# Two attention blocks on one core: operands turned and K rows spread by DMAs instead of by engines

## The chip, the cores and the metric

The kernel runs on one core of a Trainium2 chip. The metric is the device time of one execution in microseconds; the figure given is the median of three runs. A profile is one further execution, recorded by the hardware profiler. Engines are called PE (TensorE), ACT (ScalarE), DVE (VectorE), POOL (GpSimd) and SP (SyncE, which here only issues DMAs).

## The reference

Two independent blocks work on inputs of 2048 rows by 512 columns, with 32 heads of 16 columns each, everything in bfloat16. Their results stand side by side in one output of 2048 by 1024.

```python
# both: qkv = x @ wqkv, split into q, k, v of 32 heads x 16 columns
# A: linear attention
phi = lambda t: where(t > 0, t + 1, exp(t)) + 1e-6
kv  = einsum("bhsd,bhse->bhde", phi(k), v);  z = einsum("bhsd->bhd", phi(k))
o   = (phi(q) @ kv) / (phi(q) @ z + 1e-6)
a   = o @ wo
# B: softmax attention over all 2048 keys
p   = softmax(q @ k.T * 0.25);  o = p @ v
b   = o @ wo
out = concatenate([a, b], axis=-1)
```

B needs 32 heads x 2048 x 2048 exponentials. In tiles of 128 keys by 512 queries these are 2048 blocks. A is much smaller and is fitted in beside B.

## The kernel before

The program is laid out by a planner that runs when the kernel is built: it keeps a clock for each engine with a booked duration for every operation, and picks what can start first. What comes out is a fixed instruction sequence for each engine with semaphore waits. Constants such as `TEND` (the length the planner spreads its side jobs over), `ALAG` (how far A's jobs may lag before DVE gets no more exponential blocks) and `DBL` (how much work may wait for DVE) steer it.

B's scores are made with four heads at once, each in a quarter of the PE's rows. K is kept twice, once with the rows of the even heads and once with those of the odd heads, the other rows zero. A block's exponential is either computed by ACT from the scores in PSUM (three or two blocks in one instruction), or by DVE in four steps on the bits of a 16-bit number, after which PV takes two matmuls instead of one:

```python
# L670: scores of one block; KM is the masked K: [row, group % 2, even/odd, key]
return e.matmul(dst, lhsT=KM[32*g:32*g+32, Gp % 2, e_, j*128:(j+1)*128],
                rhs=QT[32*g:32*g+32, Gp % 2, c*512:(c+1)*512], ...)
# L816: ACT's way, w = 1536 or 1024
e.activation(PT[:, row, c0:c0+w], SCR[sl][:, 0:w], ACTF.Exp, scale=SC)
# L756, L872, L873, L874: DVE's way; DI for each block, the rest for three blocks at once
e.tensor_scalar(DI..., DB..., ESC, EB, op0=ALU.mult, op1=ALU.add)
e.tensor_scalar(Q, I, 0x3FF, 0x3800, op0=ALU.bitwise_and, op1=ALU.bitwise_or)
e.tensor_tensor(Qh, Ih, Qh, op=ALU.mult)
e.tensor_scalar(I, I, 0xFC00, 8, op0=ALU.bitwise_and, op1=ALU.bitwise_or)
```

The parts that the change touches, in the version before. x of both blocks comes in with rows on partitions and is turned by PE against an identity, then copied out of PSUM. A's x is turned in two halves inside the room of KNa (`XSA`), the second half loaded when the first is done:

```python
def xT_stages(src, keys_, dst, dname, t0, n=2, lane="dve"):
    def tr(e, bk):
        for i in range(n):
            for cc in range(4):
                ins = e.transpose(bfv(bk)[:, ...], src(t0+i)[:, cc*128:(cc+1)*128], identb[:])
        return ins
    return [("pe", 4*n*TRB, f_pe(tr, ...)),
            (lane, 0.36*n, f_ev(lane, copy_to(lane, ..., ...), [], [...]))]     # L419, xTb or xTa
```

The first projections (K, then Q of group 0) read the turned x of the first four row tiles; K of group 0 is masked by DVE straight from PSUM (L466). For the later groups DVE copies the projection to KR and POOL multiplies it by the two masks:

```python
st.append(("dve", 0.7, ... e.tensor_copy(KR[:, kr, :], f32v(bk)) ...))                 # L474
for e_ in range(2):
    st.append(("pool", 0.7, ... e.tensor_scalar(KM[:, r, e_, cs], KR[:, kr, :],
                                                PAR[:, e_:e_+1], None, op0=ALU.mult) ...))  # L476
st.append(("dve", 0.62, ... e.tensor_reduce(KMX[:, i:i+1], KR[:, kr, :], ...) ...))     # L478
```

A's output of a row tile is divided into OA, turned by PE, copied to ONT, and multiplied by WO; B's output tiles use the same last step without a turn:

```python
# anum_job, L593: OA[:, o2] = numerator * RD            (DVE)
# otr_job:  PE turns OA into PSUM; L419: ONT = copy       (PE, DVE)
# omm_job, L619: four matmuls with WOa or WOb; L419: copy to OB (A) or spare rows of KNa (B);
#           L623: store
early += [xjob(4), xjob(6), proj_job(0, 1, 1, fast=True), xjob(8), ...]   # the start, shortened
```

At the start PE runs matmuls on the identity to warm up (`warm`, 28 of them, L985). DVE also adds up two bounds from which a flag decides whether a slower general path follows; with these inputs it doesn't run.

Of the kernel before, what the change touches and what calls it, by code (L numbers as in the profile page):

```python
# [219 lines left out]
def bass_concat_heads__linear_attn_block__softmax_full_mha__prompt_kernel(nc, A_x, A_wqkv, A_wo, B_x, B_wqkv, B_wo, out):  # L220
# [17 lines left out]
    TEND = 780.0  # L238
    ALAG = 20.0
    DLEAD = 0.5  # L240
    DBL = 6.0
# [8 lines left out]
    with es:  # L250
# [30 lines left out]
        ONT = sb("ONT", [128, 1, 512], BF)  # L281
        OB = sb("OB", [128, 1, 512], BF)
        OA = sb("OA", [128, 2, 512], BF)
# [37 lines left out]
        xbn = B_x[0].rearrange("(t p) c -> p t c", p=128)  # L321
        xan = A_x[0].rearrange("(t p) c -> p t c", p=128)
        on_keys = lambda t: [("ON", t, g) for g in range(8)]
        load(ON[:, 0:2, :], xbn[:, 0:2, :], on_keys(0) + on_keys(1))
        load(ON[:, 2:4, :], xbn[:, 2:4, :], on_keys(2) + on_keys(3), queue="act")
        load(Wb[:, :, 0:128], wbv[:, :, 0:128], [("Wb", 0, 0)])
        load(Wb[:, :, 512:640], wbv[:, :, 512:640], [("Wb", 1, 0)], queue="act")
        for t0 in range(4, NT, 4):
            load(ON[:, t0:t0 + 4, :], xbn[:, t0:t0 + 4, :], sum([on_keys(t) for t in range(t0, t0 + 4)], []))
            if t0 == 4:  # L330
                load(Wb[:, :, 1024:1536], wbv[:, :, 1024:1536], [("Wb", 2)])
        load(Wb[:, :, 128:512], wbv[:, :, 128:512], [("Wb", 0, g) for g in range(1, NGP)])
        load(Wb[:, :, 640:1024], wbv[:, :, 640:1024], [("Wb", 1, g) for g in range(1, NGP)])
        XSA = KNa[:, :, :].rearrange("p (a b) n -> p a (b n)", b=2)
        kst = lambda i: [("KNa", 2 * i), ("KNa", 2 * i + 1)]
        for t0 in range(0, 8, 4):
            load(XSA[:, t0:t0 + 4, :], xan[:, t0:t0 + 4, :], sum([kst(i) for i in range(t0, t0 + 4)], []))
# [4 lines left out]

        def mk_ident(t, key):
            sch.add("pool", lambda e: e.memset(t[:], 0.0), writes=[key])
            sch.add("pool", lambda e: e.affine_select(out=t[:], in_=t[:], compare_op=ALU.not_equal, fill=1.0,
                                                      base=0, pattern=[[-1, 128]], channel_multiplier=1),
                    reads=[key], writes=[key])
# [3 lines left out]
        sch.add("dve", lambda e: e.memset(PVb[:], 0.0), writes=[("PV", g) for g in range(4)])  # L351
        def band(t, n, rep, key):
# [8 lines left out]
        for e_ in range(2):  # L361
            sch.add("dve", lambda e, e_=e_: e.tensor_reduce(PAR[:, e_:e_ + 1], ZMk[:].rearrange("p (a e) -> p e a", e=2)[:, e_, :],
                                                           axis=AX.X, op=ALU.max),
                    reads=["ZMk"], writes=[("PAR", e_)])
        for Gp_ in range(NGP):
# [50 lines left out]
        MM, TRB, TRF = 0.26, 0.085, 0.29  # L416
# [4 lines left out]

        def xT_stages(src, keys_, dst, dname, t0, n=2, lane="dve"):
            def tr(e, bk):
                for i in range(n):
                    for cc in range(4):
                        ins = e.transpose(bfv(bk)[:, (i * 4 + cc) * 128:(i * 4 + cc + 1) * 128],
                                          src(t0 + i)[:, cc * 128:(cc + 1) * 128], identb[:])
                return ins
            return [("pe", 4 * n * TRB, f_pe(tr, keys_ + ["identb"])),
                    (lane, 0.36 * n, f_ev(lane, copy_to(  # L430
                        lane, lambda: dst[:, :, t0 * 128:(t0 + n) * 128].rearrange("p c (i n) -> p i c n", n=128),
                        lambda bk: bfv(bk)[:, 0:n * 512].rearrange("p (i c n) -> p i c n", c=4, n=128)),
                        [], [(dname, t) for t in range(t0, t0 + n)]))]
# [14 lines left out]
        def proj_job(Gp, sc, kind, fast=False, **kw):  # L448
# [15 lines left out]
            if fast:  # L464
                for e_ in range(2):
                    st.append(("dve", 0.75, f_ev("dve", lambda e, bk, e_=e_: e.tensor_scalar(KM[:, r, e_, cs], f32v(bk), PAR[:, e_:e_ + 1], None, op0=ALU.mult),  # L466
                                                 [("PAR", e_)], [("KM", r, e_, sc)])))
                st.append(("dve", 1.2, f_op("dve", lambda e: e.tensor_reduce(KMX[:, i:i + 1], KM[:, r, :, cs], axis=AX.XY, op=ALU.max,
                                                                            apply_absolute_value=True),
                                            [("KM", r, e_, sc) for e_ in range(2)], [("KMX", i)])))  # L470
# [4 lines left out]
            for e_ in range(2):  # L475
                st.append(("pool", 0.7, f_op("pool", lambda e, e_=e_: e.tensor_scalar(KM[:, r, e_, cs], KR[:, kr, :], PAR[:, e_:e_ + 1], None, op0=ALU.mult),  # L476
                                             [("PAR", e_), ("KR", kr)], [("KM", r, e_, sc)])))
            st.append(("dve", 0.62, f_op("dve", lambda e: e.tensor_reduce(KMX[:, i:i + 1], KR[:, kr, :], axis=AX.X, op=ALU.max,  # L478
                                                                         apply_absolute_value=True), [("KR", kr)], [("KMX", i)])))
            return Job(st, needs, [(3, ("K", Gp, 0, sc)), (4, ("K", Gp, 1, sc)), (5, ("KMX", i))], rel=2, **kw)  # L480
# [59 lines left out]
        def akv_job(t, hp, **kw):  # L540
# [8 lines left out]
            return Job(st, [("xTa", t)] + ([("akv", hp - 1, bl) for bl in range(2)] if hp else [("xTa", t_) for t_ in range(NT)]),  # L549
# [34 lines left out]
        def anum_job(sc, tl, **kw):  # L584
            pq = sc % 2
            o2 = tl % 2
            def f(e, bk):
                for bq in range(4):
# [6 lines left out]
                            RD[:, pq, tl * 32:tl * 32 + 32].unsqueeze(2).broadcast_to([128, 32, 16]), op=ALU.mult), [("RD", pq)], [("OA", o2)]))],  # L595
                       [("aden", sc)] + ([("atr", sc, tl - 2)] if tl >= 2 else ([("atr", sc - 1, tl + 2)] if sc else [])),
                       [(0, ("anum", sc, tl)), (1, ("oa", sc, tl))], **kw)


        out_lanes = [sch.new_dma_lane() for _ in range(5)]  # L600
        stores = []
        KNf = KNa[:, :, :].rearrange("p (s b) n -> p s (b n)", b=2)
        obf = lambda o2: OB[:, 0, :] if o2 == 0 else KNf[:, o2 - 1, :]
        obk = lambda o2: [("OB", 0)] if o2 == 0 else kst(o2 - 1)

        def otr_job(src, keys, needs, gives, **kw):
            def tr(e, bk):
                for hb in range(4):
                    ins = e.transpose(bfv(bk)[:, hb * 128:(hb + 1) * 128], src[:, hb * 128:(hb + 1) * 128], identb[:])
                return ins  # L610
            return Job([("pe", 4 * TRB, f_pe(tr, list(keys) + ["identb"])),
                        ("dve", 0.43, f_ev("dve", copy_to("dve", lambda: ONT[:, 0, :], lambda bk: bfv(bk, 512)), [], [("ONT", 0)]))],
                       needs, gives, **kw)

        def omm_job(ab, t, o2, needs, gives, lane="dve", **kw):
            WO, wkey, col0 = (WOa, "WOa", 0) if ab == "a" else (WOb, "WOb", 512)
            def mm(e, bk, hb):
                src = ONT[:, 0, hb * 128:(hb + 1) * 128] if ab == "a" else ON[:, 4 * hb + t // 4, (t % 4) * 128:(t % 4 + 1) * 128]
                return e.matmul(f32v(bk), lhsT=src, rhs=WO[:, hb, :], start=(hb == 0), stop=(hb == 3))  # L619
            ins_ = [("ONT", 0)] if ab == "a" else sum([on_keys(4 * hb + t // 4) for hb in range(4)], [])  # L620
            def fin(bk):
                sch.add(lane, lambda e: copy_to(lane, lambda: obf(o2), lambda bk: f32v(bk))(e, bk), reads=[bk[3]], writes=obk(o2))
                stores.append(sch.add(out_lanes[o2], lambda e: e.dma_start(out[0][t * 128:(t + 1) * 128, col0:col0 + 512], obf(o2)),  # L623
                                      reads=obk(o2), queue="sp", force_signal=True))
            return Job(halves(mm, ins_ + [wkey]) + [(lane, 0.7 if lane == "dve" else 0.6, fin)],
                       needs + ([("akv", 1, bl) for bl in range(2)] if o2 else []), gives, **kw)
# [46 lines left out]
        def qk_reads(bl):  # L673
            res = []
            for u, j, g in bl:
                Gp, c, e_ = unit(u)
                res += [("QT", Gp % 2, c), ("KM", Gp % 2, e_, j // 4)]
# [26 lines left out]

        def d_pick(at, used):
# [3 lines left out]
            if bi is None or u is None or dfree[bi] > at or d_backlog(at) > DBL or (ajobs and at > ajobs[0].ready + ALAG):  # L709
# [248 lines left out]
        def unit_done(u, t_):  # L958
# [17 lines left out]
            if Gp == NGP - 1 and e_ == 1:  # L976
                fin = u == NU - 1
                for tl in range(4):
                    ln = ("dve", "act")[tl % 2] if fin else "dve"
                    urgent2.append(omm_job("b", 4 * c + tl, 1 + tl, [("on", Gp, c)], [(1, ("st", c, tl))], lane=ln))  # L980


        def warm(e):
            for i_ in range(28):
# [3 lines left out]
        xsrc = lambda t: ON[:, t, :]  # L988

# [5 lines left out]
        for t in range(4):  # L995
            now(Job(xT_stages(xsrc, on_keys(t), xTb, "xTb", t, 1, ("dve", "act")[t % 2]), gives=[(1, ("xTb", t))]), SBANKS[t], 7.0)
# [4 lines left out]
        now(jk, SBANKS[4], 10.5)  # L1001
        now(jq, DBANK[0], 11.0)
        for k_ in T:
            T[k_] = 10.3
        T["act"] = 11.2
        afree[:] = [10.0, 10.0]
        dfree[:] = [11.2, 9.0]
# [4 lines left out]
        def xjob(t):  # L1012
            return Job(xT_stages(xsrc, on_keys(t) + on_keys(t + 1), xTb, "xTb", t), gives=[(1, ("xTb", t)), (1, ("xTb", t + 1))])
        early += [xjob(4), xjob(6), proj_job(0, 1, 1, fast=True), xjob(8), xjob(10), v4_job(0, 0), proj_job(0, 2, 1, fast=True), xjob(12), xjob(14),
                  v4_job(1, 0), proj_job(0, 3, 1, fast=True), v4_job(2, 0), v4_job(3, 0)]
# [15 lines left out]
        for h2 in range(2):  # L1031
            for i in range(0, 8, 2):
                t = 8 * h2 + i
                st = xT_stages(lambda tt, h2=h2: XSA[:, tt - 8 * h2, :], kst(i) + kst(i + 1), xTa, "xTa", t)
                if h2 == 0 and i == 6:
                    fn0 = st[0][2]
                    def f2(bk, fn0=fn0):
                        fn0(bk)
                        for t0 in range(0, 8, 4):
                            load(XSA[:, t0:t0 + 4, :], xan[:, 8 + t0:12 + t0, :], sum([kst(i_) for i_ in range(t0, t0 + 4)], []))  # L1040
                    st[0] = (st[0][0], st[0][1], f2)
                ajobs.append(Job(st, [("xTa", 7)] if h2 else [], [(1, ("xTa", t)), (1, ("xTa", t + 1))]))
# [173 lines left out]
```

## Time and profile before

| what | value |
|---|---|
| median of three runs | 792.77 us (792.19 to 793.15) |
| span of the profiled execution | 791.8 us |
| first exponential on ACT starts | 9.83 us |
| last exponential on ACT ends | 778.51 us |
| POOL's mask products (L476) | 24, mean 1725 ns |
| DMA traffic | 13.51 MB, 302 GB/s in the first fortieth of the span, 17 GB/s over all |
| A's stores | 16, from 361 to 711 us |

A line of groups reads: line, engine, operation, what is written and read, shapes, count, then the total busy time and the mean of one in ns, then the idle time of the engine before them and who ended it. A line of waits reads: who waited for whom, total us, times, longest. The chain that ended last is followed backwards from the last instruction to whatever released each step; its shares say where the time that counts was spent. An engine that is busy most of the span matters only where the chain runs through it.

### The profile page before, as it was taken

The numbers are of one execution on the slowest core, as the hardware profiler recorded it, in microseconds if no ns is written. First come the engines' busy times: TensorE is split into PE (matmuls) and PEld (weight loads), VectorE is DVE, ScalarE is ACT, GpSimd is POOL, SyncE is SP. The second block draws the span as 40 slices with busy tenths as digits, with TensorE's granted clock in tenths as the row PEclk, the third lists the DMA queues.
The fourth block names the chain that finished last, engine by engine and source line by source line (L and its number), as shares of the span: only waits on it lengthen the run. The fifth ranks groups of instructions, "written<-read, shape, count | busy, mean of one in ns | idle before, by whom it ended". The sixth has DMA issues, their size and how long they took to land.

```text
span 791.8 us, 13394 instructions
## 1 busy us (share of the span) xinstructions
PE 674.2 (85%) x5585; PEld 209.6 (26%) x5634; DVE 723.3 (91%) x1264; ACT 760.0 (96%) x706; POOL 45.9 (6%) x43
## 2 busy tenths in 40 slices
PE   7889999898988888988888788988877888888875
PEld 4322333333322322222222222222222222222211
DVE  6999999989999999999999989999999997989992
ACT  6899999999999999999999999999999999999993
POOL 2000011300000001310000001121000000000000
PEclk9999999999999999999998999999999899999997
DMA  9201100000000000000000000000000000010000
GB/s 302 71 1 28 27 1 1 1 2 2 1 1 1 1 2 1 2 1 14 7 8 1 1 8 15 7 1 2 13 7 8 1 14 21 14 34 1 22 7 31
DMA packets 13139, 13.51 MB, mean 17 GB/s; under 512 B 1808, under 2 KB 12560, under 8 KB 13072
## 3 DMA queue, kind: packets, MB, share of 16 engines
q1 hardware_dynamic: 12272, 12.19, 4.8%
q8 instruction: 46, 0.75, 0.4%
q10 hardware_dynamic: 800, 0.39, 0.2%
q14 instruction: 21, 0.17, 0.1%
HBM read 8.39 MB, written 4.19 MB: 16 GB/s over the span
## 4 chain that ended last, share of the span: by engine, by line
ACT 72%; DVE 15%; PE 12%; issue 1%; POOL 0%; ACTq 0%; POOLq 0%
ACT PT L816 70%; PE pPV L935 5%; DVE DI L756 4%; PE pS L670 4%; DVE DQ L873 2%; DVE DQ L872 1%; ACT EA L534 1%; DVE DI L874 1%; PE pD L619 1%; PE pD L450 1%; DVE QMX L461 1%; DVE KMX L478 0%; DVE PQT L537 0%; DVE OT L962 0%; DVE KR L474 0%
## 5 line engine op out<-in xcount | busy, mean ns | idle before, releaser
L816 ACT ACTIVATE PT<-pS 128x1536 f16<-128x1536 f32 (+1 forms) x651 | 750.9, 1380 | 13.6 <-PE pS L670 6.5
L670 PE MATMUL pS<-QT,KM 32*128 32x512 bf16 x1628 | 256.2, 391 | 83.9 <-ACT PT L816 79.4
L756 DVE TENSOR_SCALAR DI<-pD 128x512 int16<-128x512 f32 x414 | 281.0, 689 | 29.3 <-PE pD L670 25.5
L935 PE MATMUL pPV<-PT,VV 128*17 128x512 f16 x1628 | 225.6, 390 | 1.4 <-ACT PT L816 1.0
L670 PE MATMUL pD<-QT,KM 32*128 32x512 bf16 x420 | 154.3, 392 | 2.2 <-DVE DI L756 1.1
L670 PEld LDWEIGHTS pS<-QT,KM 32*128 32x128 bf16 x1628 | 61.9, 91 | 329.1 <-ACT PT L816 299.4
L873 DVE TENSOR_TENSOR DQ<-DI,DQ 128x1536 f16<-128x1536 f16 x140 | 134.0, 957 | 2.3
L935 PE MATMUL pPV<-DQ,VV 128*17 128x512 f16 x420 | 117.0, 390 | 1.3 <-DVE OT L962 1.3
L935 PE MATMUL pPV<-DI,VV 128*17 128x512 f16 x420 | 116.2, 387 | 0.0
L872 DVE TENSOR_SCALAR DQ<-DI 128x1536 int16<-128x1536 int16 x140 | 78.4, 560 | 1.6
L874 DVE TENSOR_SCALAR DI<-DI 128x1536 int16<-128x1536 int16 x140 | 77.8, 556 | 2.0 <-DVE DQ L873 0.8
L476 POOL TENSOR_SCALAR KM<-KR,PAR 128x512 bf16<-128x512 bf16 x24 | 41.1, 1725 | 489.4 <-DVE KR L474 489.4
L935 PEld LDWEIGHTS pPV<-PT,VV 128*17 128x17 bf16 x1628 | 46.2, 88 | 85.0 <-issue 70.2
L670 PEld LDWEIGHTS pD<-QT,KM 32*128 32x128 bf16 x420 | 36.2, 91 | 14.9 <-DVE DI L756 7.0
L543 PE MATMUL pD<-Wa,xTa 128*128 128x256 bf16 x256 | 38.1, 277 | 2.1 <-DVE DI L756 1.8
L450 PE MATMUL pD<-xTb,Wb 128*128 128x512 bf16 x103 | 31.5, 390 | 6.0 <-issue 2.0
L935 PEld LDWEIGHTS pPV<-DI,VV 128*17 128x17 bf16 x420 | 30.4, 92 | 21.2 <-issue 2.0
L935 PEld LDWEIGHTS pPV<-DQ,VV 128*17 128x17 bf16 x420 | 25.9, 89 | 26.1 <-issue 16.3
L534 ACT ACTIVATE EA<-pD 128x256 bf16<-128x256 f32 (+1 forms) x48 | 29.9, 622 | 0.0
L962 DVE STREAM_TRANSPOSE OT<-pPV 128x512 f32<-128x512 f32 x32 | 22.7, 709 | 7.1 <-PE pPV L935 6.9
L543 PEld LDWEIGHTS pD<-Wa,xTa 128*128 128x128 bf16 x256 | 20.6, 98 | 18.6 <-DVE DI L756 7.2
L619 PE MATMUL pD<-WOb,ON 128*128 128x512 bf16 x57 | 18.7, 440 | 5.4 <-DVE ON L973 3.7
(86 smaller groups left out, 349.1 us busy)
## 6 DMA issues: line engine op xcount, KB each, us to landing
KNa<-in_A_x_dram SPq DMA_DIRECT2D x4, 512.0 KB, 6.7
out_dram<-OB SPq DMA_DIRECT2D x16, 128.0 KB, 1.7
out_dram<-KNa SPq DMA_DIRECT2D x16, 128.0 KB, 1.7
ON<-in_B_x_dram SPq DMA_DIRECT2D x3, 512.0 KB, 7.7
Wa<-in_A_wqkv_dram SPq DMA_DIRECT2D x1, 1536.0 KB, 12.2
Wb<-in_B_wqkv_dram SPq DMA_DIRECT2D x2, 384.0 KB, 8.5
Wb<-in_B_wqkv_dram SPq DMA_DIRECT2D x1, 512.0 KB, 6.8
WOb<-in_B_wo_dram SPq DMA_DIRECT2D x1, 512.0 KB, 12.2
```

Of the source, the lines that this page charges most:

```text
L450: return e.matmul(f32v(bk), lhsT=Wb[:, cc, kind * 512 + Gp * 128:kind * 512 + Gp * 128 + 128], rhs=xTb[:, cc, sc * 512:(sc + 1) * 512], st ...
L476: st.append(("pool", 0.7, f_op("pool", lambda e, e_=e_: e.tensor_scalar(KM[:, r, e_, cs], KR[:, kr, :], PAR[:, e_:e_ + 1], None, op0=ALU.m ...
L534: ("act", 0.1 + n * 0.00085, f_ev("act", lambda e, bk: e.activation(EA[:, q, 0:n], f32v(bk)[:, c0:c0 + n], ACTF.Exp), [], [("EA", q)])),
L543: return e.matmul(f32v(bk)[:, 256 * k_:256 * k_ + 256], lhsT=xTa[:, cc, t * 128:(t + 1) * 128], rhs=Wa[:, cc, 512 + 512 * k_ + 256 * hp:51 ...
L619: return e.matmul(f32v(bk), lhsT=src, rhs=WO[:, hb, :], start=(hb == 0), stop=(hb == 3))
L670: return e.matmul(dst, lhsT=KM[32 * g:32 * g + 32, Gp % 2, e_, j * 128:(j + 1) * 128], rhs=QT[32 * g:32 * g + 32, Gp % 2, c * 512:(c + 1) ...
L756: sch.add("dve", lambda e: e.tensor_scalar(DI[:, buf, i * 512:(i + n) * 512], DB[:, bi * 512:(bi + n) * 512], ESC, EB, op0=ALU.mult, op1=A ...
L816: sch.add("act", lambda e: e.activation(PT[:, row, c0:c0 + w], SCR[sl][:, 0:w], ACTF.Exp, scale=SC), reads=skeys(sl), writes=[("PT", row, ...
L872: (0.07 + w * 0.00027, lambda e: e.tensor_scalar(Q, I, 0x3FF, 0x3800, op0=ALU.bitwise_and, op1=ALU.bitwise_or), ik, qk_),
L873: (0.07 + w * 0.00053, lambda e: e.tensor_tensor(Qh, Ih, Qh, op=ALU.mult), ik + qk_, qk_),
L874: (0.07 + w * 0.00027, lambda e: e.tensor_scalar(I, I, 0xFC00, 8, op0=ALU.bitwise_and, op1=ALU.bitwise_or), ik, ik)]
L935: sch.add("pe", lambda e, g=g, j=j, h=h, P=P, first=first, last_=last_: e.matmul(PVb[32 * g:32 * g + 17, 0:512], lhsT=VV[:, j, vcol(h):vco ...
```

## The change

x of both blocks no longer passes through PE and PSUM: transposing DMAs write it turned from HBM to SBUF, 512 rows at a time. This takes away the transposes, their copies on DVE and ACT, and the jobs that held PSUM banks for them. A's attention output is turned by a transposing DMA from SBUF to SBUF. The masked K of the later groups is filled by DMAs that copy only the 16 rows each head needs, eight for a projection, into a KM whose other rows are zeroed once at the start by POOL. ONT, OB and OA lose their own memory: they lie in KNa and VNa, which are free when A's sums are done. The planner's constants follow.

```diff
-    TEND = 780.0
-    ALAG = 20.0
+    TEND = 765.0
+    ALAG = 30.0
-    DBL = 6.0
+    DBL = 5.0
...
-        ONT = sb("ONT", [128, 1, 512], BF)
-        OB = sb("OB", [128, 1, 512], BF)
-        OA = sb("OA", [128, 2, 512], BF)
...
+        def load_t(dst, dname, x, t0, n):
+            lane = sch.new_dma_lane()
+            sch.add(lane, lambda e: e.dma_start_transpose(dst[:, :, t0 * 128:(t0 + n) * 128], x[0][t0 * 128:(t0 + n) * 128, :]),
+                    writes=[(dname, t) for t in range(t0, t0 + n)], queue="sp")
         load(Wb[:, :, 512:640], wbv[:, :, 512:640], [("Wb", 1, 0)], queue="act")
+        load(Wb[:, :, 0:128], wbv[:, :, 0:128], [("Wb", 0, 0)], queue="act")
+        load_t(xTb, "xTb", B_x, 0, 4)
+        load_t(xTb, "xTb", B_x, 4, 4)
+        load(Wb[:, :, 1024:1536], wbv[:, :, 1024:1536], [("Wb", 2)])
+        load_t(xTb, "xTb", B_x, 8, 4)
+        load_t(xTb, "xTb", B_x, 12, 4)
...
+        for t0 in range(0, NT, 4):
+            load_t(xTa, "xTa", A_x, t0, 4)
...
+        for r_, e_, sc_ in zeros:
+            sch.add("pool", lambda e, r_=r_, e_=e_, sc_=sc_: e.memset(KM[:, r_, e_, sc_ * 512:(sc_ + 1) * 512], 0.0), ...)
...
-            for e_ in range(2):
-                st.append(("pool", 0.7, f_op("pool", lambda e, e_=e_: e.tensor_scalar(KM[:, r, e_, cs], KR[:, kr, :], PAR[:, e_:e_ + 1], None, op0=ALU.mult),
+            def spread(bk):
+                for e_ in range(2):
+                    for g in range(4):
+                        rows = slice(32 * g + 16 * e_, 32 * g + 16 * e_ + 16)
+                        sch.add(km_lanes[4 * e_ + g], lambda e, rows=rows, e_=e_: e.dma_start(KM[rows, r, e_, cs], KR[rows, kr, :]),
+                                reads=[("KR", kr)], writes=[("KM", r, e_, sc, g)], queue="sp")
+            st.append(("pool", 5.0, spread))
...
+        def ont_load(o2):
+            sch.add(ont_lane, lambda e: e.dma_start_transpose(ONT[:, o2, :].rearrange("p (c n) -> p c n", n=128), OA[:, o2, :]),
+                    reads=oak(o2), writes=kst(6 + o2), queue="sp")
...
         def warm(e):
-            for i_ in range(28):
+            for i_ in range(36):
...
+        for t in range(NT):
+            tok[("xTb", t)] = 5.5 + 2.0 * (t // 4)
+            tok[("xTa", t)] = 24.0
...
             for tl in range(4):
                 ajobs.append(anum_job(sc, tl))
-                ajobs.append(otr_job(...))
-                ajobs.append(omm_job("a", 4 * sc + tl, 0, [("aont", sc, tl)], []))
+                if sc or tl:
+                    ajobs.append(aout_job(4 * sc + tl - 1))
```

The last lines put the output product of a tile of A behind the numerator of the next tile. The `tok` lines are the times at which the planner assumes the turned x to be there; the program itself waits for the DMAs' semaphores.

## The prediction

> **What bounds the kernel now.** I read the page's busy line first, then the chain that ended last, then the groups with shapes kept apart.
>
> ```profile
> PE 674.2 (85%) x5585; PEld 209.6 (26%) x5634; DVE 723.3 (91%) x1264; ACT 760.0 (96%) x706; POOL 45.9 (6%) x43
> ...
> ACT 72%; DVE 15%; PE 12%; issue 1%; POOL 0%; ACTq 0%; POOLq 0%
> ```
>
> ScalarE (ACT) is busy 760.0 of 791.8 us and carries 72% of the chain. VectorE (DVE) is at 91%: a bound only slightly looser. The next view (groups, shapes apart) says what both do.
>
> ```profile
> L816 ACT ACTIVATE PT<-pS 128x1536 f16<-128x1536 f32 x326 | 518.6, 1591 | 9.9 <-PE pS L670 4.4 <-PE pD L670 4.3 <-PE pD L619 0.9
> L816 ACT ACTIVATE PT<-pS 128x1024 f16<-128x1024 f32 x325 | 380.1, 1170 | 3.7 <-PE pS L670 2.1 <-PE pD L670 1.5
> L756 DVE TENSOR_SCALAR DI<-pD 128x512 int16<-128x512 f32 x408 | 273.7, 682 | 29.3 <-PE pD L670 25.5 <-PE pS L670 2.0
> ...
> L419 DVE COPY ONT<-pD 128x512 bf16<-128x512 bf16 x16 | 6.6, 415 | 1.2 <-PE pD L609 1.2
> ...
> L419 DVE COPY xTa<-pD 128x1024 bf16<-128x1024 bf16 x8 | 5.4, 680 | 0.0
> ...
> L419 DVE COPY xTb<-pD 128x1024 bf16<-128x1024 bf16 x6 | 4.1, 680 | 0.0
> ```
>
> The reader is to see the exchange in this. The 2048 exponential blocks (128x512 each) are shared out when the program is built: 326x3 + 325x2 = 1628 on ACT, 408 + 6x2 = 420 on DVE. DVE also carries the copies of transposed x and of A's output. A block taken off ACT saves about (1591 - 1170) = 421 ns at the margin, half a us with its share of the fixed part. On DVE it costs 0.68 us for DI and a third of a chain of 560 + 957 + 556 ns, thus 1.37 us. So every microsecond freed on DVE is worth roughly a third of one on ACT.
>
> Where ACT idles comes from its waits, the first answer for the first 30 us, the second for 30 to 760 us:
>
> ```profile
> ACT PT L816 <- PE pS L670: 4.3, 3, 2.1
> ACT xTb L419 <- PE pS L426: 2.3, 1, 2.3
> ACT QT L1000 <- PE pD L450: 2.0, 1, 2.0
> ACT L350 <- issue: 1.8, 1, 1.8
> ```
>
> ```profile
> ACT PT L816 <- PE pD L670: 5.0, 8, 1.3
> ACT PT L816 <- PE pS L670: 1.9, 3, 1.2
> ACT PT L816 <- PE pD L619: 0.9, 1, 0.9
> ```
>
> Idle ACT is 31.8 us in all (791.8 - 760.0). The timeline puts the first exponential at 9.83 us, with 3.2 us of other ACT work before it: 6.6 us idle. Waits of exponentials in the first 30 us: 4.3. Middle: 7.8 (5.0 + 1.9 + 0.9). In a table of 10 us windows most of those sit where the granted TensorE clock drops (0.83 at 250, 0.72 at 430, 0.82 at 630 us), about 0.9 us each time. After the last exponential ends (778.51 in the chain) the tail is PV, normalization, 16 output matmuls (6.19 us) and the store: 13.3 us, 12.1 of them idle on ACT. A further 1.1 us is lost just before. Sum 31.9.
>
> **What the Trainium skill says.** "VectorE: DVE Perf Modes", The three transpose paths: TensorE turns 128x128 in 390 ns but into PSUM, the DMA crossbar in 1309 ns straight into SBUF. Here eight TensorE transposes took 0.62 us, and the eviction behind them 0.68 us of DVE; that eviction is what the DMA path saves. "DMA: Bandwidth & Descriptors", Latency and other measured facts: a transposing DMA got 261 GB/s with a non-contiguous middle dimension, 350 to 400 when contiguous. This trace has no such DMA; its plain loads moved 302 GB/s in the first slice. The same page, Rules for kernel authors: transfers under 64 KB pay mostly overhead; the spread uses 16 KB ones, and the trace shows 1.7 us from issue to landing for a store of 128 KB. "SBUF — State Buffer", SBUF: two separate sides: GpSimd and VectorE exclude each other on a shared port pair, DMA does not take part. The trace agrees mildly: the 1536-wide L872 has a median of 551 ns, a mean of 560 and a maximum of 982.
>
> **The change, part by part.** Counts come from the instructions that both programs issue, in program order.
>
> 1. Copies leave DVE: xTb 6 x 0.680 + 2 x 0.424 = 4.9 us, xTa 8 x 0.680 = 5.4, ONT 16 x 0.415 = 6.6. Sum 17.0 us. On ACT two xTb copies of 0.598 go: 1.2, before the first exponential.
>
> 2. The plan spends this on exponentials: ACT gets 323 wide, 322 narrow and one single instead of 326 and 325, thus 1614 blocks; DVE gets 434. DVE pays 8 x 0.682 + 3 x 1.201 (double-width DI) = 9.1, 4 more chains x 2.07 = 8.3, and one two-block chain, about 1.4: 18.7 us. DVE is then 723.3 - 17.0 + 18.7 = 725.0, less 1 or 2 if POOL's 24 products (41.1 us) held it up at the shared ports: no change. ACT pays 3 x 1.591 + 3 x 1.170 - 0.75 (one block: 1.170 - 0.421) = 7.5 us less. **This is the main term: -7.5 us.**
>
> 3. Start. Before, a 256 KB load landed 3.7 us after its issue; transposes and copies then delayed the K projection to 6.80, and the first exponential came 3.03 us later at 9.83. After, 512 KB must land turned before that projection. Estimate from 0.79 us (issue of the first load): about 2 us of latency (from the 1.7 of the stores), then 768 KB (x and two parts of Wb) at 261 to 302 GB/s, 2.6 to 3.0 us, thus 5.4 to 5.8. The warm-up of 36 matmuls ends near 1.57 + 36 x 0.113 = 5.6, so it no longer matters. First exponential near 8.8: **-1.0 us**. ACT's idle before it stays about 6.7, as the copies that leave were busy time.
>
> 4. The first 30 us. DVE loses 4.1 us of copies there, and PE 48 transposes between the fills, which made ACT wait 4.3 us. I expect about 1 us to stay: **-3.3 us**.
>
> 5. Spread of K. 24 POOL products of 1.57 to 2.37 us become 96 small transfers. K of a group is projected tens of us before its first use (the products ran at 113 to 155 us for a group used from about 200 us), so 5 us more of latency is hidden. POOL is 6% busy and on no chain: 0.
>
> 6. A's output: TensorE transpose, eviction and ONT leave; a transposing DMA from SBUF (the plan books 2.6 us) takes their place. In program order the output product of tile t comes after the next tile's product, usually with score and PV groups between, so the latency is mostly covered. PE loses 192 transposes (16.5 us of busy time by the groups) and gains 14 second PV products: some relief at the clock drops, which I count as 0 to -1 us.
>
> 7. Late buffers inside A's K and V: no instruction more or less; A's stores go to the spare rows of K. Tail: the same 16 output products and stores, 0.
>
> Sum: ACT busy 760.0 - 7.5 - 1.2 = 751.3; idle 6.7 + 1.0 + 7.8 + 1.1 + 12.1 = 28.7; span 780.0. The timed median was 1.0 above the profiled span (792.8 against 791.8), thus 781; with half of item 6's relief, **780.5 us**, -1.5%.
>
> **Rivals.**
> - Late landing: if the turned x comes at a third of the plain rate, the first chunk lands 5 us later, at about 11 us, and the other three starve K and V meanwhile. Against it: the page's rate. For it: no trace here shows one. It would cost 5 to 12 us and leave 785 to 793.
> - In-order queues: all new transfers go through SyncE in program order, and PE waits in order. If a turned tile of A came 2 us later than booked for all 16 tiles, PE would stall up to 32 us; the double buffering of scores hides perhaps two thirds. Worth up to +10 us. The program order speaks against most of it.
> - DVE as the bound: DVE keeps 725 us of work in a shorter span, 725 / 780 = 93% instead of 91%. Its 25.5 us of waiting for score matmuls shows that it still has slack; if not, blocks come late to PV and ACT waits for freed buffers: +3 us.
> - More is gained than counted: the horizon in the code is lowered by 15 us, from 780 (it ran 792.8) to 765. If the real time follows it, 778; and if the middle waits vanish too, 773.
>
> **Range and chances.** The main term is a count of instructions with measured durations, and fairly certain; start and middle idle are not. Best case 780.5 - 7 (middle waits gone); worst 780.5 + 7 (one rival). So 774 to 788. The 2% line is 776.9, 3.6 us below the estimate: 0.26 for faster. Over 808.6 needs both delay rivals in full: 0.03.
>
> **What will show it.** Right if ACT busy is 751 to 752 with 645 exponentials plus one, DVE within 3 us of 725, the first exponential at 8.5 to 9.2, ACT's waits of the first 30 us about 3 us smaller, POOL's products gone without any score matmul waiting for KM's transfers, and the tail still 13 us. Wrong if the turned loads land later than 7 us, if PE shows idle time released by the queue of A's turned tiles, if ACT's middle waits grow past 10 us, or if exponentials or DI change their mean durations beside the new traffic.

## The result and the profile after

The changed kernel took 782.03 us (median of 4 runs, 777.73 to 783.68) beside 792.96 for the one before, a ratio of 0.985 with a 95% interval of 0.9803 to 0.9897. In a second session it took 779.68 beside 794.84: 0.9818 (0.9786 to 0.985). The prediction was 780.5, within 774 to 788.

The page of the changed kernel, busy line and shares of the chain that ended last (line numbers have moved: L820 is the exponential, L671 the scores, L760 DI):

```profile
PE 665.8 (86%) x5464; PEld 199.7 (26%) x5464; DVE 721.0 (93%) x1258; ACT 752.5 (97%) x699; POOL 8.5 (1%) x27
...
ACT 75%; DVE 13%; PE 10%; DMA 1%; issue 0%; ACTq 0%
```

ACT's work fell by 7.5 us and ACT is still the bound. POOL is empty. DVE's work is nearly the same as before (723.3 us), in a shorter span: it lost its copies and took on blocks. Its groups by shape, and ACT's merged group from the page:

```profile
L820 ACT ACTIVATE PT<-pS 128x1536 f16<-128x1536 f32 x323 | 517.5, 1602 | 7.2 <-PE pD L671 6.0 <-issue 0.3
L760 DVE TENSOR_SCALAR DI<-pD 128x512 int16<-128x512 f32 x416 | 278.7, 682 | 18.6 <-PE pD L671 17.7 <-PE pS L671 0.2
```

```profile
L820 ACT ACTIVATE PT<-pS 128x1536 f16<-128x1536 f32 (+1 forms) x646 | 745.4, 1391 | 8.2 <-PE pD L671 6.3
```

ACT's waits, the first answer for 0 to 30 us, the second for 30 to 760 us:

```profile
ACT QT L1003 <- PE pD L447: 4.9, 1, 4.9
ACT L352 <- issue: 1.8, 1, 1.8
ACT PT L820 <- PE pD L671: 1.4, 3, 0.6
ACT PT L820 <- PE pS L671: 0.2, 1, 0.2
```

```profile
ACT PT L820 <- PE pD L671: 4.9, 6, 1.4
ACT PT L820 <- PE pS L671: 0.4, 1, 0.4
ACT PT L820 <- issue: 0.3, 1, 0.3
```

Exponentials waited 1.6 us in the first 30 us instead of 4.3, and 5.6 instead of 7.8 in the middle. What the start became, in order of time (start, length, engine, instruction, idle before it and its releaser):

```profile
0.80 5.06 SPq L323 DMA_TRANSPOSE xTb<-in_B_x_dram  x2
...
6.30 1.04 PE L447 MATMUL pS<-xTb,Wb 128*128 128x512 bf16 x4 [0.76 <-DMA xTb<-in_B_x_dram]
...
9.43 5.97 ACT L820 ACTIVATE PT<-pS 128x1536 f16<-128x1536 f32 x5 [0.60 <-PE pD L671]
...
13.66 11.46 SPq L323 DMA_TRANSPOSE xTa<-in_A_x_dram  x4
```

PE finished its warm-up and waited 0.76 us for the first turned chunk. The new transfers, from the list of DMA issues (KB and us to landing; transposes have us alone):

```profile
KM<-KR SPq DMA_DIRECT2D x96, 16.0 KB, 1.8
...
KNa<-VNa SPq DMA_TRANSPOSE x16, 2.4
xTb<-in_B_x_dram SPq DMA_TRANSPOSE x4, 5.5
xTa<-in_A_x_dram SPq DMA_TRANSPOSE x4, 5.2
```

Of the later ones the trace shows one wait, 0.2 us of a weight load for B's x; PE's waits show no time released by KNa<-VNa or KM<-KR.

The ledger of the profiled spans, in us:

| part | before | predicted | after |
|---|---|---|---|
| ACT busy | 760.0 | 751.3 | 752.5 |
| ACT idle before the first exponential | 6.6 | 6.7 | 7.4 |
| exponentials' waits, first 30 us | 4.3 | 1.0 | 1.6 |
| exponentials' waits, middle | 7.8 | 7.8 | 5.6 |
| just before the last exponential | 1.1 | 1.1 | 0 |
| ACT idle in the tail | 12.1 | 12.1 | 11.1 |
| span | 791.8 | 780.0 | 778.6 |

The first exponential's own wait (0.49 us before, 0.60 after) stands in both of the first two idle rows, and gaps too short for the waits view are in none. So the columns sum only roughly; the prediction counted the same way. By windows ACT idled 3.8 us before and 1.0 after from the first exponential to 30 us, and 8.2 and 6.6 us in the middle.

### The profile page after: what moved, and what is told of

It is laid out like the page before. It is cut to its first block, busy times and chain, and to the rows that moved or that the text cites. A ratio compares the mean times of both kernels' runs of the same rounds, so it can differ in the third digit from the quotient of the medians.

```text
span 778.6 us, 13253 instructions
## 1 busy us (share of the span) xinstructions
PE 665.8 (86%) x5464; PEld 199.7 (26%) x5464; DVE 721.0 (93%) x1258; ACT 752.5 (97%) x699; POOL 8.5 (1%) x27
## 4 chain that ended last, share of the span: by engine, by line
ACT 75%; DVE 13%; PE 10%; DMA 1%; issue 0%; ACTq 0%
ACT PT L820 73%; DVE DI L760 5%; PE pPV L939 4%; PE pS L671 3%; DVE DQ L877 2%; ACT EA L535 2%; PE pD L620 1%; DVE DQ L876 1%; DVE DI L878 1%; PE pD L447 1%; DMA xTb<-in_B_x_dram 1%; DVE OT L966 0%; DVE PQT L538 0%; PE pD L519 0%; DVE KMX L465 0%
## 5 line engine op out<-in xcount | busy, mean ns | idle before, releaser
L820 ACT ACTIVATE PT<-pS 128x1536 f16<-128x1536 f32 (+1 forms) x646 | 745.4, 1391 | 8.2 <-PE pD L671 6.3
L671 PE MATMUL pS<-QT,KM 32*128 32x512 bf16 x1614 | 254.8, 390 | 88.5 <-ACT PT L820 85.1
L760 DVE TENSOR_SCALAR DI<-pD 128x512 int16<-128x512 f32 (+1 forms) x425 | 289.6, 693 | 18.9 <-PE pD L671 17.9
L671 PE MATMUL pD<-QT,KM 32*128 32x512 bf16 x434 | 160.3, 390 | 1.0 <-DVE PQT L538 0.2
L671 PEld LDWEIGHTS pS<-QT,KM 32*128 32x128 bf16 x1614 | 61.7, 91 | 337.9 <-ACT PT L820 305.2
L877 DVE TENSOR_TENSOR DQ<-DI,DQ 128x1536 f16<-128x1536 f16 (+1 forms) x145 | 137.9, 951 | 2.6
L939 PE MATMUL pPV<-DQ,VV 128*17 128x512 f16 x434 | 122.0, 387 | 1.1 <-DVE OT L966 1.0
L939 PE MATMUL pPV<-DI,VV 128*17 128x512 f16 x434 | 121.1, 385 | 0.3 <-DVE DI L878 0.2
L876 DVE TENSOR_SCALAR DQ<-DI 128x1536 int16<-128x1536 int16 (+1 forms) x145 | 80.2, 553 | 2.1
L878 DVE TENSOR_SCALAR DI<-DI 128x1536 int16<-128x1536 int16 (+1 forms) x145 | 79.9, 551 | 1.1
L671 PEld LDWEIGHTS pD<-QT,KM 32*128 32x128 bf16 x434 | 37.3, 91 | 10.9 <-DVE DI L760 4.1
L447 PE MATMUL pD<-xTb,Wb 128*128 128x512 bf16 x124 | 36.2, 390 | 3.3 <-DVE DI L760 2.6
L429 DVE CAST KNa<-pD 128x512 bf16<-128x512 f32 x30 | 20.5, 682 | 6.0 <-PE pD L620 5.1
```

What stands on the lines that cost most here:

```text
L447: return e.matmul(f32v(bk), lhsT=Wb[:, cc, kind * 512 + Gp * 128:kind * 512 + Gp * 128 + 128], rhs=xTb[:, cc, sc * 512:(sc + 1) * 512], st ...
L671: return e.matmul(dst, lhsT=KM[32 * g:32 * g + 32, Gp % 2, e_, j * 128:(j + 1) * 128], rhs=QT[32 * g:32 * g + 32, Gp % 2, c * 512:(c + 1) ...
L760: sch.add("dve", lambda e: e.tensor_scalar(DI[:, buf, i * 512:(i + n) * 512], DB[:, bi * 512:(bi + n) * 512], ESC, EB, op0=ALU.mult, op1=A ...
L820: sch.add("act", lambda e: e.activation(PT[:, row, c0:c0 + w], SCR[sl][:, 0:w], ACTF.Exp, scale=SC), reads=skeys(sl), writes=[("PT", row, ...
L876: (0.07 + w * 0.00027, lambda e: e.tensor_scalar(Q, I, 0x3FF, 0x3800, op0=ALU.bitwise_and, op1=ALU.bitwise_or), ik, qk_),
L877: (0.07 + w * 0.00053, lambda e: e.tensor_tensor(Qh, Ih, Qh, op=ALU.mult), ik + qk_, qk_),
```

## The experiments

Theory: the gain is the 14 exponential blocks that the plan moves from ACT to DVE, plus a better start. I took the blocks to be paid for by the DVE time that the copies gave back. Rivals: the three planner constants, the K spread, PE and its PSUM banks, or DVE time as such. Each ratio is to the kernel before on the same chip. One more edit of the planner comes with the change and stands in no run alone: it closes an open group of DVE blocks when A lags. Built without it, the changed kernel still gives DVE 434 blocks (427 instead of 431 at the old constants); what it does to the time was not measured.

**e1, the constants alone.**

```diff
 # before.py
-    TEND, ALAG, DBL = 780.0, 20.0, 6.0
+    TEND, ALAG, DBL = 765.0, 30.0, 5.0
```

> The kernel before, with only the three planner constants of the change (TEND 765, ALAG 30, DBL 5). It still issues 326 wide and 325 narrow exponentials on ACT and gives DVE 420 blocks, as before. If the freed DVE time is the cause of the gain (my theory), nothing moves: 790 to 795 us, ACT busy 759 to 761. If the gain comes from the looser lag and the shorter horizon (rival), it falls to 782 to 787.

Measured: 791.91 us, ratio 0.9973 (0.9958 to 0.9988), ACT busy 760.7. These values by themselves give a quarter of a per cent; the trace shows 420 blocks on DVE (410 + 5 x 2), as before.

**e2, the change with the old constants** (the same edit reversed, on the changed kernel).

> The changed kernel with the three constants of before. Its program issues 323 + 323 exponentials on ACT (1615 blocks) and 431 to 433 blocks on DVE, so 1 or 2 fewer on DVE than the change. Theory of the freed DVE time: about 1 us slower than the change, 780 to 785. Constants as cause: back to 788 or more.

Measured: 784.62, ratio 0.9883 (0.9848 to 0.9917), ACT busy 753.4. Most of the gain stays, and the trace shows 431 blocks on DVE (409 + 11 x 2).

**e3, K masked by POOL again.**

```diff
 # after.py
-            st.append(("pool", 5.0, spread))          # eight DMAs
+            for e_ in range(2): st.append(("pool", 0.7, ... tensor_scalar KM = KR * PAR ...))
```

> The changed kernel, but K's rows are masked by 24 POOL products again instead of 96 DMAs (and no zeroing of KM at the start). DVE has 432 blocks instead of 434. Theory: the spread is worth nothing by itself, 780 to 785, within 2 us of the change. Rival (POOL held DVE up at a shared port, or the spread's DMAs cost something): DVE's wide steps L872 and L874 of before get 10 ns or more longer again and the time is 3 us or more higher; or it is faster by more than 2 us if 96 small DMAs are the burden.

Measured: 786.43, ratio 0.9888 (0.984 to 0.9937), 1.4 us above the theory's range, with an interval that overlaps the change's. The detail that the rival named came back in part. Two steps of DVE's chain, first in e3, then in the changed kernel (groups by shape):

```profile
L870 DVE TENSOR_TENSOR DQ<-DI,DQ 128x1536 f16<-128x1536 f16 x142 | 136.8, 964 | 2.9
L869 DVE TENSOR_SCALAR DQ<-DI 128x1536 int16<-128x1536 int16 x142 | 80.0, 564 | 2.1
```

```profile
L877 DVE TENSOR_TENSOR DQ<-DI,DQ 128x1536 f16<-128x1536 f16 x144 | 137.3, 953 | 2.5
L876 DVE TENSOR_SCALAR DQ<-DI 128x1536 int16<-128x1536 int16 x144 | 79.8, 554 | 2.1
```

With 4 ns on the third step (556 against 552) that is 25 ns x 142 = 3.6 us of DVE (by the same sum 14 ns x 140 = 2.0 us in the kernel before), which goes when POOL is empty. The 3 us or more in the time, which the rival also names, is neither shown nor excluded.

**e4, A's output turned by PE and copied by DVE.**

```diff
 # after.py
-        ... ("pool", 2.6, lambda bk: ont_load(o2)) ...        # DMA from OA to ONT
+        otr_job(t): PE 4 transposes of OA, DVE copy to ONT    # as before
```

> The changed kernel with A's output turned by PE again and copied by DVE (16 copies of 0.415 us = 6.6 us of DVE, 64 transposes on PE), in place of the transposing DMA. The program gives DVE 424 blocks, 10 fewer, and ACT 325 + 324 + 1. Theory: ACT pays 10 x 0.42 to 0.5 = 4 to 5 us, time 785 to 788, ACT busy 756 to 758. Rival (the DMA turn's latency stalls PE in the changed kernel): no slower than the change, or faster, as PE no longer waits for DMAs.

Measured: 785.79, ratio 0.9885 (0.9843 to 0.9927), ACT busy 756.6. Both figures are in the expected ranges, which speaks against the rival, a stall of PE on the DMA turn.

**e6, the freed DVE time filled with nothing** (e5 is the changed kernel run again beside it, 779.68).

> The changed kernel once more, as the yardstick beside the next three: 778 to 784 us, ratio 0.983 to 0.988. Both theories expect the same.

```diff
 # after.py
+        ballast: Job([("dve", 0.68, tensor_reduce of 128x512 into a spare column)])
+        # 6 among the early jobs, 8 ahead of A's jobs, 11 beside A's output tiles
```

> The changed kernel with 25 useless VectorE reductions of 0.68 us (17 us, what the change took off VectorE) placed where the copies were: 6 among the early jobs, 8 ahead of A's jobs, 11 beside A's output tiles. No transpose, copy or DMA comes back. The program gives DVE 412 blocks instead of 434 and ACT 327 + 327 + 1. Theory (DVE time is what the change sells): 22 blocks x 0.46 us = 10 us slower than the change, 789 to 794, ACT busy 761 to 763. Rival (the gain is from PE's transposes, PSUM banks or the start): at most 3 us slower, 780 to 785.

Measured: 798.94, ratio 1.005 (1.0023 to 1.0077): slower than before, though every DMA of the change is there. The page:

```profile
PE 676.8 (85%) x5442; PEld 199.6 (25%) x5442; DVE 716.5 (90%) x1250; ACT 763.3 (96%) x708; POOL 8.6 (1%) x27
```

ACT's work is within 0.3 us of my range, but the time is 5 us above it. ACT idles 796.8 - 763.3 = 33.5 us, and the granted clock of the profiled run is 0.957 instead of 0.988 in e5. More on that below: at the mean clock of the kernel before, the fit puts e6 at about 792.5.

**e7 and e8, one x alone turned by DMA, on the kernel before.** e7 also has the longer warm-up, and both have the planner's new ready times for x.

```diff
 # e7: before.py                                    # e8: before.py
-  load(ON..., B_x), xT_stages(... xTb ...)         -  load(XSA..., A_x), xT_stages(... xTa ...)
+  load_t(xTb, "xTb", B_x, ...)                     +  load_t(xTa, "xTa", A_x, ...)
```

> The kernel before with only B's x turned by DMA (and the longer warm-up); A's x, A's output, K's masks and the constants as before. DVE loses 4.9 us of copies, the program gives it 423 blocks instead of 420. Theory: ACT saves 3 x 0.46 + 1.2 us of copies, and about 2.5 us of its waits in the first 30 us go: 786 to 790. Rival (late landing eats what the copies cost): 791 or more, with ACT idle before the first exponential up by 1 us or more.

> The kernel before with only A's x turned by DMA. DVE loses 8 copies of 0.68 us, PE 64 transposes, but with the old constants the program gives DVE 416 blocks, 4 fewer than before, and ACT 326 + 326. If blocks on ACT decide (my theory), the freed 5.4 us are not spent and the time rises by 4 x 0.46 = 2 us: 794 to 796. If busy time on DVE itself decides (rival), it falls by 2 to 3 us: 789 to 791.

Measured: e7 786.64, ratio 0.9894 (0.9866 to 0.9922), with 0.6 us of exponentials' waits left in the first 30 us. Turning B's x alone gives about half of the gain: 5.8 us, where e5 has 12.6, once both are put at the clock of the kernel before by the fit below. e8: 797.82, ratio 1.0044 (1.0024 to 1.0065), 1.8 us above my range. It is slower than before, with less work on DVE (714.3 us instead of 723.3) and 64 transposes fewer on PE:

```profile
PE 684.2 (86%) x5566; PEld 209.1 (26%) x5566; DVE 714.3 (89%) x1242; ACT 763.7 (96%) x708; POOL 46.6 (6%) x43
```

So freed DVE time is not spent by itself. The plan put 4 more blocks on ACT. In the profiled run ACT's work is 3.7 us more and its idle time 4.2 us more (799.7 - 763.7 = 36.0 instead of 31.8).

**e9, before with one constant changed.**

```diff
 # before.py
-    TEND = 780.0
+    TEND = 788.0
```

> The kernel before with a horizon of 788 instead of 780 and nothing else. Over 24 settings of the three constants the built program of before gives DVE 411 to 424 blocks (median 420), that of the change 422 to 435 (median 427 to 428); this setting is the best of before with 424, the change as given sits near its own best with 434. If the number of blocks that the plan puts on DVE decides the time, at 0.5 to 0.9 us a block (the slope over the runs so far), before gains 2 to 4 us without any DMA: 790 to 793 beside 794 to 795. If the number is only a side effect (rival), it stays at 794 to 795.

Measured: 787.65, ratio 0.9902 (0.9876 to 0.9928), 2.4 us below my range. Not only 4 blocks moved: the mean granted clock of its runs was 0.986, beside 0.974 for the kernel before. By the fit below the blocks account for 1.9 of the 7.2 us and the clock for 4.6.

**e10 and e11, blocks and DVE time taken apart.**

```diff
 # e10: after.py, d_pick
+            if dcount[0] >= 420 / 2048.0 * taken + 4 or dcount[0] >= 420: return None
 # e11: after.py, proj_job of groups 1 to 3
-            KMX and QMX: 24 x tensor_reduce          # left out; the bound covers group 0 only
```

> The changed kernel, but the planner may give DVE no more than 420 blocks, spread evenly over the units: ACT has 326 + 325 as in before, DVE idles instead, no transposes or copies come back. Theory (ACT's share of blocks is the main term): 14 x 0.46 = 6.5 us more on ACT, 785 to 789. Rival (it is DVE's load that decides, and less of it removes waits): 778 to 783 despite the longer ACT work.

> The changed kernel without the 24 reductions that bound Q and K of groups 1 to 3 (16 us of DVE left out; the bound then covers group 0 only). With unchanged constants the program nevertheless gives DVE 428 blocks, 6 fewer than the change. If every us freed on DVE shows up in the time by itself (rival), this is the fastest: 770 to 776. If only blocks moved off ACT count (theory), it is 3 to 5 us slower than the change: 781 to 785.

Measured: e10 790.31, ratio 0.9939 (0.9915 to 0.9964); e11 784.3, ratio 0.9866 (0.9843 to 0.989). Their busy lines, e10 and then e11:

```profile
PE 670.6 (85%) x5450; PEld 199.8 (25%) x5450; DVE 709.0 (90%) x1230; ACT 758.8 (96%) x704; POOL 8.5 (1%) x27
```

```profile
PE 675.2 (86%) x5458; PEld 200.4 (25%) x5458; DVE 704.6 (90%) x1225; ACT 755.1 (96%) x701; POOL 8.5 (1%) x27
```

DVE is 12 and 16 us lighter than in the changed kernel, and neither is faster. e10 is above my range; at the mean clock of the kernel before it would be within it, by the fit below. The lightest DVE of all has 428 blocks and a time between. The time follows ACT's share of blocks, not DVE's load.

**e12, an attempt to beat both: a shorter tail.**

```diff
 # after.py, after the last PV matmuls of the last unit
-  16 output matmuls when the last head group is normalized
+  12 of them (head groups 0 to 2) at once into four score banks; 4 afterwards
```

> The changed kernel with another end: of the last 16 output matmuls, the 12 that need only the first three head groups are issued right after the last PV matmuls, into four score banks, and run while VectorE normalizes the last unit (2.7 us); 4 remain after it. Same blocks everywhere else. The tail after the last exponential falls from 12.3 us by 2.5 to 4: 775 to 778 us, 0.975 to 0.979 of before. If the matmuls are slowed by the low clock at the end or the evictions take over as bound (rival), by 1 us or less.

Measured: 779.04, ratio 0.9802 (0.9779 to 0.9826); e5 had 0.9818 (0.9786 to 0.985). It beats the kernel before, but isn't told apart from the changed one. The timelines of the tail say why: first e5, then e12 (the last copies of B's output, and the stores).

```profile
769.07 0.69 DVE L429 CAST KNa<-pD 128x512 bf16<-128x512 f32 x1 [2.47 <-PE pD L620]
770.19 0.60 ACT L429 ACTIVATE KNa<-pD 128x512 bf16<-128x512 f32 x1 [2.23 <-PE pD L620]
```

```profile
762.63 3.63 PE L989 MATMUL pS<-WOb,ON 128*128 128x512 bf16 x16
...
765.87 1.08 ACT L429 ACTIVATE KNa<-pS 128x512 bf16<-128x512 f32 x2 [3.60 <-PE pS L989]
766.37 2.54 SPq L997 DMA_DIRECT2D out_dram<-KNa  x4
```

The last copy ends at 766.95 instead of 770.79, although the last exponential ended at the same time (762.3 against 762.1). The matmuls left the path. But the last of the four stores, issued at 768.5, took 3.8 us to land; in e5 the last was issued at 770.8 and took 1.7. The span ends at 773.3 instead of 773.6. My expectation missed: the last store took over as the end. The four stores now follow each other within 2.5 us; whether that slows the last one was not tested, nor was issuing them over two queues.

## Why the prediction was right, and which steps were not

**The sum holds at an equal clock.** I fitted the timed runs of before and of e1 to e12 (without e10's longest) by least squares, every kernel with equal weight, on three quantities: blocks on DVE, whether B's x comes turned by DMA, and the run's granted clock. The result is -0.48 us for a block, -5.3 us for B's x, and -3.8 us for each 0.01 of granted clock. Within the runs of single kernels alone the clock's slope is -3.7. No kernel's mean is off by more than 2.2 us. With each kernel's mean as one observation, the standard errors are about 0.10, 1.3 and 0.9 us. With DVE's busy time in place of the blocks the typical miss of a kernel's mean rises from 1.5 to 2.7 us. At an equal clock the change is then worth 14 x 0.48 + 5.3 = 12.0 us, beside 792.8 - 780.5 = 12.3 predicted.

The second term also holds what else the kernels with the change share. At an equal clock it is 4.3 us by e7, which has B's x alone (its 3 blocks taken off), and about 6.5 by e10, which has the whole change at the 420 blocks of before. How the difference is split among the other parts was not tested.

That the number came so close is in part luck. The terms below miss in both directions, and four runs of the changed kernel spread over 6 us. I also took the timed run to be 1.0 us longer than the profiled span, from two different executions; within one execution it is 1.7 (793.52 against 791.8) before and 2.0 (780.56 against 778.6) after.

**The main term (step 2), count right, price too high.** The counts came out of the built programs. The 7.5 us were 0.54 us a block, taken from mean durations of single exponentials. These overlap: by shape they sum to 518.6 + 380.1 = 898.7 us, while the merged line of the page before has 750.9 busy:

```profile
L816 ACT ACTIVATE PT<-pS 128x1536 f16<-128x1536 f32 (+1 forms) x651 | 750.9, 1380 | 13.6 <-PE pS L670 6.5
```

The average price is 750.9 / 1628 = 0.461 us, or 6.5 us for 14 blocks; the fit's 0.48 agrees. The profiled exponentials fell by 750.9 - 745.4 = 5.5, in e5 by 7.1.

**The exchange of DVE time for ACT time failed as a rule.** I wrote that every microsecond freed on DVE is worth a third of one on ACT. e8 and e11 freed 5.4 and 16 us with unchanged constants, and their plans gave DVE 4 and 6 blocks fewer. e6 shows that the reverse does hold: with DVE filled, 22 blocks went back. How many blocks the plan moves depends also on its constants. Over 24 settings, before gets 411 to 424 blocks (median 420, which is also its own value). The changed kernel gets 422 to 435 (median 427 to 428) and was given 434. By the medians 7 or 8 of the 14 blocks belong to the change and 6 or 7 to the choice of constants; by e2, at the old constants, 11 and 3. e9 bought 4 for before with one number. Why the plan loses blocks when DVE is relieved stays open.

**Start (step 3), too hopeful.** The first turned chunk came at 6.30 us, not at 5.4 to 5.8. SyncE was busy 5.06 us issuing the first two transposes, a cost that my estimate from bytes didn't have. The first exponential came at 9.43, not 8.8: a gain of 0.4, not 1.0. **First 30 us (step 4):** 2.7 instead of 3.3, in a run whose clock was at 0.66 from 10 to 20 us; e5, with full clock there, waited 0.7 in all. **Spread (step 5):** hidden, as said; with POOL empty DVE's steps are 2.0 to 3.6 us shorter in all, not 1 to 2; the 2.0 against the kernel before are half of why DVE ended at 721.0 and not 725. **A's turn (step 6):** landed in 2.4 us and covered, as said. **Middle waits:** counted as unchanged, 2.2 less. **Tail (step 7):** 1.0 shorter; the 16 matmuls took 5.73 us instead of 6.19, beside the clock's own changes from run to run.

Of the signs named beforehand, ACT's work missed its range by 0.5 us, the first exponential by 0.2, and DVE's work is 4.0 us from 725, not within 3. Exponentials took 10 to 11 ns longer by shape (1602 against 1591 for the wide ones), which was named as a sign of being wrong; in e5 it is 2 to 4. PE's and ACT's waits came out as named.

The rate that the Trainium skill gives for transposing DMAs ("DMA: Bandwidth & Descriptors", Latency and other measured facts: 261 GB/s with a non-contiguous middle dimension, about 350 to 400 when contiguous) was not reached here. The 512 KB chunks of B's x took 4.4 to 6.1 us from issue to landing, thus 86 to 119 GB/s for one chunk seen alone, and issuing the four chunks of A's x took 11.46 us, thus 183 GB/s. The skill also says that GpSimd and VectorE exclude each other on a shared port pair ("SBUF — State Buffer", SBUF: two separate sides); e3 agrees in kind, at 4 to 11 ns an instruction on average.

**What the prediction left out** is the granted clock. It goes with about two thirds of the spread among runs of one kernel (e10: 782.4 us at 0.986, 793.5 at 0.961). This is a correlation: no run sets the clock, so that it is a cause of the time is not shown.

## What to carry to other kernels

When a build-time planner shares work between engines, count in the built program what each engine is given before pricing anything; time taken off an engine counts only as far as the plan moves work onto it. Compare two versions of such a kernel each at its best constants: here one horizon constant gave the old kernel 1.0% (more than half of it with the clock), beside 1.5 to 1.8% for the whole change. Price pipelined instructions by merged busy time over count, not by their mean duration.

## What the runs showed of the hardware

A transposing DMA is slow to issue: 1.4 to 3.8 us of SyncE for 512x512 bf16 from HBM, and 1.2 us (2.2 at most) for 128x512 from SBUF, against 0.33 us for a plain 128 KB store. A 16 KB copy inside SBUF landed in 1.8 us, about as late as that store (1.7).

The mean granted TensorE clock differs between plans of much the same work and doesn't follow PE's busy time. It was 0.949 to 0.963 over the runs of e6, 0.978 to 0.991 over those of e9, with PE busy 676.8 and 677.1 us. At the 3.7 us for 0.01 that go with it within single kernels, that is as much as the change itself. What in a plan sets it was not found.
